# The last four F blocks of half one as one Strassen group, and their row tiles kept in DRAM until half two

## The chip, the cores and the metric

The kernel runs on one core of a Trainium2 chip. The metric is the time of one execution in microseconds of the device. The times below are medians of several executions; the profile is of one execution. Of the engines, PE multiplies matrices (PEld loads its weights), DVE and ACT work on SBUF and PSUM, POOL (GpSimd) on SBUF alone, and SP issues DMAs; ACT and POOL can issue DMAs too.

## The reference, cut to what matters

```python
x = A_x                                     # (1, 2048, 576), float32
xn = layernorm(x)
s = A_ref(xn, A_wqkv, A_w_phi, A_wo)        # linear attention, 32 heads of 18
b = (silu(xn @ B_w_gate) * (xn @ B_w_up)) @ B_w_down   # 576 -> 4608 -> 576
return x + s * silu(b)
```

The change touches the line of b (its last product, by B_w_down) and the last one. Every product runs in a split form: each float32 operand is a high part and a rest, and three products (high-high, high-rest, rest-high) are summed.

## The kernel before, in words

The 2048 rows are two halves of 1024 (`i` = 0 and 1, "half one" and "half two"). The 4608 columns of the gate are 36 F blocks of 128 (`NF`). The first part of the kernel normalizes, does the attention (its result s goes to `s_dram`) and, beside it, six F blocks of gate and up for both halves, whose h goes to `h_dram`. The second part, from about 500 us on, is one loop over `units`: for each half its 36 blocks in a fixed order, `n` being the place in it. Half two begins with a stored block, and every fourth of its first blocks is a stored one.

**Gate and up.** `gate_up` makes h of one block for the 1024 rows, as two pieces h[0] and h[1] of 512, with seven Strassen-Winograd products, `product` (L570), over the operand tiles X00 to X13. It has four PSUM tiles: two `px`, one `py`, one `pw`. ACT copies px out (`snap`, L599), DVE adds pw to such a copy (L604), ACT takes the Silu of py (L615) and px (L625), and DVE multiplies to h[1] (L626) and h[0] (L630, which is put into the list `anchor`). Products S3, A22 and S4 write px and pw again after those copies and additions. `operands(1)` reloads all seven X tiles for half two.

**Down.** h of all blocks is multiplied by rows of B_w_down and summed over the blocks. Two blocks ("a pair") and two row pieces form 2 x 2 matrices, and the product of a pair is done by seven Strassen products p1 to p7 (`strassen`), each with its own sum: `acc[:, 0..3]`, the two of `pair_sums` (P1 and P6, in an X tile) and `last_sum` (P7). Normally two pairs, four blocks, form a group, so that one PSUM tile `pd` takes both pairs before it is added to its sum (L794; the first group of a half is copied by ACT instead). Matmuls of the down part are L669. `combine` (L811) turns the seven sums into the four quarters of the result, in place in `acc`: part 0 after p6, part 1 after p3.

The last four blocks of a half (n = 32 to 35) are different. Blocks 32 and 33 are a Strassen group of a single pair. `combine` follows. Blocks 34 and 35 are multiplied in the plain form (`plain`, L672): for each of eight row tiles of 128 rows ACT copies the tile's sum from `acc` into `pd` (L690), PE adds the plain products, and ACT takes the Silu out of `pd` (L698). In half one that Silu goes back into `acc` and from there by a DMA from ACT's queue to `y_dram` (L699). In half two `finish` multiplies by s, adds x and stores.

The row tiles of half one are finished in half two, one behind every second block from n = 15 on, by `late_finish` (L645): y from `y_dram` into the tile `ts` (one buffer), s and x into `ld` (two buffers), DVE multiplies and adds (L653, L654) after the latest anchor, SP stores (L655).

**The order.** The down work lies in `queue`. `gate_up` calls `fill` at four points between its products, a stored block twice; `fill` runs items of the queue until it has done `share` pairs' worth (2, from n = 31 on 3) and leaves `LAG` = 3 behind. `look` prepares the next items (subtractions on POOL, splits into high part and rest on ACT and DVE). Over this program order a planner puts the instructions of each engine in an order of its own, by costs that it assumes and by priorities; on the chip every engine then takes its instructions in that order and waits on semaphores. `tc.issue_after(x)` keeps instructions behind x in that order.

Of the kernel before, what the change touches and what calls it, by code (L numbers as in the profile page):

```python
# [9 lines left out]
F32 = mybir.dt.float32  # L10
F32R = mybir.dt.float32r
AF = mybir.ActivationFunctionType
# [5 lines left out]
P = 128  # L18
# [3 lines left out]
HT = HS // P  # L22
NF = F // P
HALF = D // 2
# [22 lines left out]
def gated_hedgehog_kernel(ctx: ExitStack, tc, x, w_qk, w_v, w_phi, wo, w_gu, w_tail, w_down, ident_in, mask_in, out):  # L47
# [5 lines left out]
    nc = tc.nc  # L53
# [3 lines left out]
    def split(hi, lo, src):  # L57
        nc.scalar.copy(hi, src)  # L58
        nc.vector.tensor_sub(lo, src, hi)  # L59
# [7 lines left out]
    dram = ctx.enter_context(tc.tile_pool(name="dram", bufs=1, space=bass.MemoryType.DRAM))  # L67
# [6 lines left out]
    w_dram = dram.tile([NF - EARLY, P, 7, 4, P], F32, name="w_dram")  # L74
    t_dram = dram.tile([TAILS, 4, 3, 32, 7, P], F32, name="t_dram")
    a_dram = dram.tile([3, P, 5, BT], F32, name="a_dram")
    y_dram = dram.tile([HT, P, 2, HALF], F32, name="y_dram")

    def block(t):
        return t // HT, (t % HT) // 4, slice((t % 4) * P, (t % 4 + 1) * P)  # L80
# [42 lines left out]
    with ExitStack() as att:  # L123
# [8 lines left out]
        with ExitStack() as kst:  # L132
# [4 lines left out]
            with ExitStack() as pst:  # L137
# [104 lines left out]
                for n in range(6):  # L242
                    k, c = divmod(n, 3)
# [265 lines left out]
    acc = fp.tile([P, 4, HT // 2, HALF], F32, name="acc")  # L509
# [68 lines left out]
    def split_h(src):  # L578
        t = fp.tile([P, 2, BT], F32R, name="hh", bufs=4)
        split(t[:, 0], t[:, 1], src)  # L580
        return t

    def stored(src, fill):
        h = h_tile()
        for r in range(2):
            nc.sync.dma_start(h[r], src[:, r * BT:(r + 1) * BT])
        for _ in range(2):
            fill()
        return h
# [44 lines left out]
    def halves_of(ap):  # L634
        return ap.rearrange("p (a n) -> p a n", a=2)

    def finish(t, k, pd, sx, eng):
        r0 = HS + t * P
        a = acc[:, t // 4 * 2:t // 4 * 2 + 2, t % 4][:, k]
        nc.scalar.activation(a, pd, AF.Silu)  # L640
        nc.vector.tensor_mul(a, a, halves_of(sx[:, 0])[:, k])  # L641
        eng.tensor_add(a, a, halves_of(sx[:, 1])[:, k])  # L642
        nc.sync.dma_start(halves_of(of[r0:r0 + P, :])[:, k], a)

    def late_finish(t):  # L645

        y = fw.tile([P, D], F32, name="ts")
        sx = fw.tile([P, 2, D], F32, name="ld", bufs=2)
        r = slice(t * P, t * P + P)
        nc.sync.dma_start(halves_of(y), y_dram[t])  # L650
        for m, src in enumerate((s_dram, xf)):
            nc.sync.dma_start(sx[:, m], src[r, :])
        nc.vector.tensor_mul(y, y, sx[:, 0])  # L653
        nc.vector.tensor_add(y, y, sx[:, 1])  # L654
        nc.sync.dma_start(of[r, :], y)  # L655

    def final_rows(n):
        name = ("X02", "X00", "X01", "X03")[3 - n]
        t = xpool.tile([P, 2, 2, D], F32, name=name)
        r = slice(HS + 2 * n * P, HS + 2 * n * P + 2 * P)  # L660
        for m, src in enumerate((s_dram, xf)):
            nc.sync.dma_start(t[:, :, m], src[r, :].rearrange("(a p) n -> p a n", p=P))
        return t

    def three(ps, hs, ws, first):
        for n, (h, w) in enumerate((a, b) for b, a in zip(ws, hs)):
            mm = ((h[0], w[0]), (h[0], w[1]), (h[1], w[0]))
            for m, (l, r) in enumerate(mm):
                nc.tensor.matmul(ps, l, r, start=first and n == 0 and m == 0, stop=n == len(hs) - 1 and m == 2,  # L669
                                 skip_group_check=True)  # L670

    def plain(i, fs, hr, final):  # L672

        ws = []

        def weights():
            raw = fw.tile([P, 2, D], F32, name="ld", bufs=2)
            for n, f in enumerate(fs):
                nc.sync.dma_start(raw[:, n], w_down[f * P:(f + 1) * P, :])
            for n in range(2):  # L680
                w = fq.tile([P, 2, D], F32R, name="dw", bufs=3)
                split(w[:, 0], w[:, 1], raw[:, n])
                ws.append(w)

        def tile_of(t, hs):
            pd = fps.tile([P, 2, 512], F32, name="pd", bufs=2)
            fine = i == 1 and t == HT // 2 - 1
            c = slice(t % 4 * P, t % 4 * P + P)
            a2 = acc[:, t // 4 * 2:t // 4 * 2 + 2, t % 4]
            nc.scalar.copy(pd[:, :, 0:HALF], a2)  # L690
            for k in range(2):
                n = slice(k * HALF, (k + 1) * HALF)
                three(pd[:, k, 0:HALF], [(h[:, 0, c], h[:, 1, c]) for h in hs], [(w[:, 0, n], w[:, 1, n]) for w in ws],
                      False)
                if fine:
                    finish(t, k, pd[:, k, 0:HALF], final[t // 2][:, t % 2], nc.vector)
            if i == 0:
                nc.scalar.activation(a2, pd[:, :, 0:HALF], AF.Silu)  # L698
                nc.scalar.dma_start(y_dram[t], a2)  # L699
            elif not fine:  # L700
                finish(t, slice(0, 2), pd[:, :, 0:HALF], final[t // 2][:, t % 2], (nc.vector, nc.gpsimd)[t % 2])

        for r in (1, 0) if i else (0, 1):
            hs = []

            def prep(r=r, hs=hs):
                if not ws:
                    weights()
                hs += [split_h(hr[n][r]) for n in range(2)]

            queue.append([2, prep, [(2, lambda t=4 * r + t, hs=hs: tile_of(t, hs)) for t in range(4)]])
# [3 lines left out]
    def pair_sums(i):  # L715
        if (i, 0) not in extra:
            extra[i, 0] = xpool.tile([P, 2, HT // 2, HALF], F32, name="X02")
        return extra[i, 0]

    def last_sum(i):  # L720
        if (i, 1) not in extra:
            extra[i, 1] = fp.tile([P, HT // 2, HALF], F32, name="sx")
        return extra[i, 1]
# [87 lines left out]
    def combine(i, part, final):  # L811
        P1, P6, P7 = pair_sums(i)[:, 0], pair_sums(i)[:, 1], last_sum(i)
        C11, C12, C21, C22 = (acc[:, n] for n in range(4))
        if part == 0:
            nc.vector.tensor_add(P6, P6, P1)
            nc.vector.tensor_add(P7, P7, P6)
            nc.gpsimd.tensor_add(P6, P6, C22)
            nc.vector.tensor_sub(C21, P7, C21)
            nc.vector.tensor_add(C22, C22, P7)
            for k in (3, 2)[0:2 * i]:  # L820
                final[k] = final_rows(k)
        else:
            nc.gpsimd.tensor_add(C11, C11, P1)
            nc.vector.tensor_add(C12, C12, P6)  # L824
            for k in (1, 0)[0:2 * i]:
                final[k] = final_rows(k)

# [6 lines left out]
    queue, anchor, share = [], [], [2]  # L834
# [31 lines left out]
    est.close()  # L866
    fq = ctx.enter_context(tc.tile_pool(name="fq", bufs=1, reuse_waits="tile"))
    fps = ctx.enter_context(tc.tile_pool(name="fps", bufs=1, space=PSUM, reuse_waits="tile"))
    finals, late = {}, list(range(HT))
    for i, n, f in units:  # L870
        share[0] = 2 if n < RUSH else 3
        if i == 1 and n == 0:
            xo = operands(1)
        if f >= EARLY:
            w = kept.pop() if i and kept else ready.pop(0)
            if (i, f) == (0, NF - 1):
                kept.append(w)
            if todo and (i, f) != (0, NF - 1):
                ready.append(gate_up_weights(*todo.pop(0)))
        h = stored(h_dram[i, f], fill) if f < EARLY else gate_up(w, xo, fill, (i, f) == (0, EARLY))  # L880
        if n % 2 == 0:
            g = {"f": (f, units[units.index((i, n, f)) + 1][2]), "h": [h]}
            if n % 4 == 0:
                group = []
            if n < NF - 2:
                group.append(g)
        else:
            g["h"].append(h)
        if n >= NF - 2:
            if n % 2:  # L890
                plain(i, g["f"], g["h"], finals)
            continue
        if n >= NF - 4 or n % 4 > 1:
            strassen(i, group, n % 2, n < 4)
        if n % 2 == 0:
            continue
        if i and n >= 15 and late:
            with tc.issue_after(anchor[-1].ins):
                late_finish(late.pop(0))
        if n == NF - 3:  # L900
            for k in range(2):
                queue.insert(len(queue) - 2 + 3 * k,
                             [0, None, [(0, lambda i=i, k=k: combine(i, k, finals))]])
# [37 lines left out]
```

## Time and profile before

| | |
|---|---|
| median of three runs | 1647.22 us (1646.2 to 1649.27) |
| the profiled execution's own time | 1648.95 us |
| its span, first to last instruction | 1647.0 us |
| mean granted clock of PE | 0.998 |
| PE busy | 1613.3 us, 98% of the span |
| DVE, ACT, POOL busy | 1178.3, 715.3, 618.7 us |
| matmuls L669 (128 x 288) | 3048 |
| moved by DMA | 264.68 MB, mean 161 GB/s |

The profile is of one execution. Busy time is the union of an engine's instructions; idle time before an instruction is put down to what released it. A matmul's duration is its latency, and matmuls overlap, so their rate is read from one start to the next.

### The profile page before, as it was taken

To read this page: it belongs to the slowest core of one execution; us is meant where nothing else is said; L and a number is where in the kernel's file an instruction comes from. 1 tells how busy PE (TensorE), PEld (TensorE's weight loads), DVE (VectorE), ACT (ScalarE), POOL (GpSimd) and SP (SyncE) were. 2 spreads that over 40 slices of the span, in tenths; PEclk is the share of its full clock that TensorE was granted. 3 is DMA by queue.
4 is the path that set the end of the run, shared out by engine and by line. 5 is a ranking of instruction groups with operands and counts; after the bars stand their busy time and mean duration, and the time that the engine had idled before them with its cause. 6 is when DMAs were issued, how large, how long until landed. Compare 5 with 4: busy or idle time off the path is not lost.

```text
span 1647.0 us, 25211 instructions
## 1 busy us (share of the span) xinstructions
PE 1613.3 (98%) x9441; PEld 1436.0 (87%) x9441; DVE 1178.3 (72%) x1722; ACT 715.3 (43%) x1389; POOL 618.7 (38%) x660
## 2 busy tenths in 40 slices
PE   6999999999999999999999999999999999999998
PEld 5899998999987688888888888888888888888887
DVE  7677758989852476887887778844666677566578
ACT  5533345443431365444544445445433333333334
POOL 3467500343202344554554453422333244133132
PEclk9999999999999999999999999999999999999999
DMA  9623303343218545455455454495545556455435
GB/s 285 215 79 103 116 34 105 92 142 117 74 45 289 204 159 191 161 175 181 171 176 176 173 179 164 132 361 170 164 127 161 174 167 216 152 183 187 141 114 172
DMA packets 118107, 264.68 MB, mean 161 GB/s; under 512 B 12418, under 2 KB 48386, under 8 KB 116194
## 3 DMA queue, kind: packets, MB, share of 16 engines
q1 hardware_dynamic: 107628, 247.44, 45.0%
q0 software_dynamic: 3072, 11.02, 2.4%
q10 hardware_dynamic: 7286, 4.63, 0.9%
q8 instruction: 74, 1.21, 0.3%
q14 instruction: 47, 0.39, 0.1%
HBM read 164.21 MB, written 98.83 MB: 160 GB/s over the span
## 4 chain that ended last, share of the span: by engine, by line
PE 66%; DVE 2%; issue 1%; DMA 0%; POOL 0%; ACT 0%; SPq 0%; DVEq 0%; POOLq 0%
PE pd L669 24%; PE px L570 23%; PE pw L570 11%; PE py L570 6%; PE pe L92 2%; DVE acc L641 0%; DVE hh L59 0%; DMA hb<-h_dram 0%; DMA X<-s_dram 0%; DVE dw L59 0%; DVE w L59 0%; DVE ha L630 0%; DVE acc L642 0%; DVE s L604 0%; DVE acc L824 0%
## 5 line engine op out<-in xcount | busy, mean ns | idle before, releaser
L669 PEld LDWEIGHTS pd<-dw,hh 128*128 128x128 f32 x3048 | 431.9, 189 | 28.4 <-DVE dw L59 5.4
L669 PE MATMUL pd<-dw,hh 128*128 128x288 f32 x3048 | 448.3, 297 | 5.7 <-DVE dw L59 4.0
L570 PE MATMUL px<-X,w 128*128 128x512 f32 x1440 | 373.5, 393 | 1.5 <-ACT w L58 1.0
L570 PEld LDWEIGHTS px<-X,w 128*128 128x128 f32 x1440 | 261.3, 188 | 52.7 <-ACT s L599 3.5
L570 PE MATMUL pw<-X,w 128*128 128x512 f32 x720 | 185.5, 393 | 0.0
L570 PEld LDWEIGHTS pw<-X,w 128*128 128x128 f32 x720 | 134.7, 188 | 30.3 <-DVE s L604 0.3
L604 DVE TENSOR_TENSOR s<-pw,s 128x512 f32<-128x512 f32 x120 | 82.5, 687 | 102.6 <-ACT s L599 91.8
L92 PE MATMUL pe<-X,wh 128*128 128x512 f32 (+1 forms) x480 | 152.1, 400 | 1.7 <-POOL X L199 0.7
L794 DVE TENSOR_TENSOR acc<-pd,acc 128x576 f32<-128x576 f32 x128 | 96.1, 751 | 77.9 <-PE pd L669 77.8
L599 ACT COPY s<-px 128x512 f32<-128x512 f32 x120 | 70.3, 586 | 155.1 <-PE px L570 154.9
L59 DVE TENSOR_TENSOR hh<-ha,hh 128x512 fp32r<-128x512 f32 x140 | 115.5, 850 | 14.8 <-ACT hh L58 13.8
L58 ACT CAST hh<-ha 128x512 fp32r<-128x512 f32 x140 | 82.7, 619 | 95.4 <-PE pd L669 72.2
L92 PE MATMUL p<-KVWH,X 128*128 128x288 f32 (+1 forms) x640 | 123.6, 298 | 0.4 <-DVE phi L274 0.4
L766 POOL TENSOR_TENSOR hb<-hb 128x512 f32<-128x512 f32 x34 | 46.4, 1364 | 164.1 <-DVE hb L626 163.6
L92 PEld LDWEIGHTS pe<-X,wh 128*128 128x128 f32 (+1 forms) x480 | 88.5, 189 | 19.7 <-DVE h L120 1.5
L92 PEld LDWEIGHTS p<-KVWH,X 128*128 128x128 f32 (+1 forms) x640 | 100.5, 188 | 1.1 <-issue 0.8
L59 DVE TENSOR_TENSOR w<-ld,w 128x512 fp32r<-128x512 f32 (+1 forms) x90 | 76.2, 847 | 31.9 <-ACT w L58 30.5
L570 PE MATMUL px<-X,wt 96*128 96x512 f32 x240 | 94.8, 395 | 0.0
L570 PE MATMUL py<-X,w 128*128 128x512 f32 x360 | 94.0, 394 | 0.1
L779 POOL TENSOR_TENSOR ha<-ha 128x512 f32<-128x512 f32 x34 | 52.4, 1556 | 109.5 <-DVE hh L59 109.5
L58 ACT CAST w<-ld 128x512 fp32r<-128x512 f32 (+1 forms) x90 | 49.4, 549 | 87.5 <-POOL ld L560 55.2
L753 POOL TENSOR_TENSOR h<-ha,hb 128x512 f32<-128x512 f32 x34 | 45.4, 1334 | 100.7 <-DVE ha L630 66.6
(181 smaller groups left out, 3044.1 us busy)
## 6 DMA issues: line engine op xcount, KB each, us to landing
w_dram<-w SPq DMA_DIRECT2D x87, 512.0 KB, 2.8
w<-w_dram SPq DMA_DIRECT2D x87, 512.0 KB, 4.4
wt<-t_dram SPq DMA_DIRECT2D x59, 336.0 KB, 3.5
ld<-in_B_w_gu SPq DMA_DIRECT2D x30, 512.0 KB, 4.5
X<-sum_dram SPq DMA_DIRECT2D x8, 1280.0 KB, 6.8
rt<-in_B_w_down SPq DMA_DIRECT2D x33, 288.0 KB, 3.9
rb<-in_B_w_down SPq DMA_DIRECT2D x33, 288.0 KB, 4.0
w_dram<-w SPq DMA_DIRECT2D x29, 256.0 KB
```

The lines of the kernel that those rows point to most:

```text
L58: nc.scalar.copy(hi, src)
L59: nc.vector.tensor_sub(lo, src, hi)
L92: nc.tensor.matmul(ps, l, r, start=n == 0, stop=n == len(pairs) - 1)
L570: nc.tensor.matmul(ps, l, r, start=first and n == 0, stop=last and n == len(mm) - 1, skip_group_check=True)
L599: nc.scalar.copy(t, ps)
L604: nc.vector.tensor_add(t, ps, t)
L669: nc.tensor.matmul(ps, l, r, start=first and n == 0 and m == 0, stop=n == len(hs) - 1 and m == 2, skip_group_check=True)
L753: sub(s, g["h"][0][0], g["h"][0][1])
L766: nc.gpsimd.tensor_add(a21, a21, g["h"][1][1])
L779: sub(a12, a12, g["h"][0][0])
L794: nc.vector.tensor_add(a2, pd[:, :, 0:HALF], a2)
```

## The change

In half one the blocks n = 32 to 35 become one ordinary Strassen group of two pairs. `plain` is then used in half two alone. `combine` of half one moves behind that group, and its result, the sums themselves without a Silu, is stored by `keep`: four DMAs of 128 x 1152 from GpSimd's queue, two behind part 0 and two behind part 1. `y_dram` is laid out as `acc` is. In half two `late_rows` loads a row tile's y, s and x one step (two blocks) ahead of its `late_finish`, which now takes the Silu on ACT, outside of the `issue_after` that holds the multiplication and the addition.

```diff
-    y_dram = dram.tile([HT, P, 2, HALF], F32, name="y_dram")
+    y_dram = dram.tile([4, P, 4 * HALF], F32, name="y_dram")
...
-    def late_finish(t):
-
+    def late_rows(t):
         y = fw.tile([P, D], F32, name="ts")
         sx = fw.tile([P, 2, D], F32, name="ld", bufs=2)
-        r = slice(t * P, t * P + P)
-        nc.sync.dma_start(halves_of(y), y_dram[t])
+        r, c = slice(t * P, t * P + P), slice(t % 4 * HALF, (t % 4 + 1) * HALF)
+        nc.sync.dma_start(halves_of(y), y_dram[t // 4 * 2:t // 4 * 2 + 2, :, c].rearrange("k p n -> p k n"))
         for m, src in enumerate((s_dram, xf)):
             nc.sync.dma_start(sx[:, m], src[r, :])
-        nc.vector.tensor_mul(y, y, sx[:, 0])
-        nc.vector.tensor_add(y, y, sx[:, 1])
+        return r, y, sx
+
+    def late_finish(r, y, sx):
+        nc.scalar.activation(y, y, AF.Silu)
+        with tc.issue_after(anchor[-1].ins):
+            nc.vector.tensor_mul(y, y, sx[:, 0])
+            nc.vector.tensor_add(y, y, sx[:, 1])
         nc.sync.dma_start(of[r, :], y)
...
-            if i == 0:
-                nc.scalar.activation(a2, pd[:, :, 0:HALF], AF.Silu)
-                nc.scalar.dma_start(y_dram[t], a2)
-            elif not fine:
+            if not fine:
                 finish(t, slice(0, 2), pd[:, :, 0:HALF], final[t // 2][:, t % 2], (nc.vector, nc.gpsimd)[t % 2])
...
     def combine(i, part, final):
...
+        def keep(*ns):
+            for n in ns:
+                nc.gpsimd.dma_start(y_dram[n], acc[:, n].rearrange("p t n -> p (t n)"))
+
         if part == 0:
...
             nc.vector.tensor_add(C22, C22, P7)
+            if i == 0:
+                keep(2, 3)
...
             nc.vector.tensor_add(C12, C12, P6)
+            if i == 0:
+                keep(0, 1)
...
-            if n < NF - 2:
+            if i == 0 or n < NF - 2:
                 group.append(g)
...
-        if n >= NF - 2:
+        if i and n >= NF - 2:
             if n % 2:
-                plain(i, g["f"], g["h"], finals)
+                plain(g["f"], g["h"], finals)
             continue
-        if n >= NF - 4 or n % 4 > 1:
+        if n % 4 > 1 or (i and n >= NF - 4):
             strassen(i, group, n % 2, n < 4)
         if n % 2 == 0:
             continue
-        if i and n >= 15 and late:
-            with tc.issue_after(anchor[-1].ins):
-                late_finish(late.pop(0))
-        if n == NF - 3:
+        if i and n >= 13:
+            if rows:
+                late_finish(*rows.pop())
+            if late:
+                rows.append(late_rows(late.pop(0)))
+        if n == (NF - 1, NF - 3)[i]:
```

More of the change, by code (lines that the diff above doesn't have):

```diff
@@ L670, in three, with plain @@
                                  skip_group_check=True)
-    def plain(i, fs, hr, final):
+    def plain(fs, hr, final):
         ws = []
@@ L686, in tile_of @@
             pd = fps.tile([P, 2, 512], F32, name="pd", bufs=2)
-            fine = i == 1 and t == HT // 2 - 1
+            fine = t == HT // 2 - 1
             c = slice(t % 4 * P, t % 4 * P + P)
@@ L696, in tile_of @@
                     finish(t, k, pd[:, k, 0:HALF], final[t // 2][:, t % 2], nc.vector)
-            if i == 0:
-                nc.scalar.activation(a2, pd[:, :, 0:HALF], AF.Silu)
-                nc.scalar.dma_start(y_dram[t], a2)
-            elif not fine:
+            if not fine:
                 finish(t, slice(0, 2), pd[:, :, 0:HALF], final[t // 2][:, t % 2], (nc.vector, nc.gpsimd)[t % 2])
-        for r in (1, 0) if i else (0, 1):
+        for r in (1, 0):
             hs = []
@@ L868, in gated_hedgehog_kernel @@
     fps = ctx.enter_context(tc.tile_pool(name="fps", bufs=1, space=PSUM, reuse_waits="tile"))
-    finals, late = {}, list(range(HT))
+    finals, late, rows = {}, list(range(HT)), []
     for i, n, f in units:
```

## The prediction

> **What bounds the kernel now.** I read the page first, then a table of busy time by stretch, then what PE waits for, then the timelines of the places that the change touches.
>
> ```profile
> span 1647.0 us, 25211 instructions
> PE 1613.3 (98%) x9441; PEld 1436.0 (87%) x9441; DVE 1178.3 (72%) x1722; ACT 715.3 (43%) x1389; POOL 618.7 (38%) x660
> ...
> 1068.00:1136.00 68.00, 68.00 (x368) 59.33 (x367) 33.61 (x46) 33.97 (x62) 16.47 (x12) 1.00 0.85 304
> 1136.00:1590.00 454.00, 454.00 (x2507) 401.56 (x2506) 293.60 (x426) 174.83 (x347) 142.23 (x119) 1.00 0.52 162
> ...
> PE pd L669 <- DVE X L794: 0.4, 1, 0.4
> ```
>
> The two middle rows are the table by stretch (length; then busy time and count of PE, PEld, DVE, ACT, POOL). From 1068 to 1136 us, where half one goes over into half two, PE is busy all 68.00 us, and in half two from 1136 to 1590 all 454.00. The last row is all that PE waits for between 900 and 1300 in the view of waits. So PE is the bound: a matmul that goes is worth its time, and a delay of another engine costs nothing until PE waits for it, and from there on all of it.
>
> **Matmuls removed.** In the plain form the last pair of F blocks of half one costs 96 matmuls of 288 columns (8 row tiles, 2 column halves, 2 blocks, 3 terms). As the second pair of a Strassen group it adds 84 (7 products, 4 row tiles, 3 terms). 12 go, and the order in which the changed kernel is built shows just that.
>
> ```profile
> 1090.81 1.76 PE L669 MATMUL pd<-dw,hh 128*128 128x288 f32 x12
> 1092.40 1.53 PE L570 MATMUL px<-X,w 128*128 128x512 f32 x6
> 1094.01 1.76 PE L669 MATMUL pd<-dw,hh 128*128 128x288 f32 x12
> 1052.53 1.06 PE L669 MATMUL pd<-dw,hh 128*128 128x288 f32 x6 [0.44 <-DVE X L794]
> 1085.91 3.22 PEld L669 LDWEIGHTS pd<-dw,hh 128*128 128x128 f32 x24 [0.33 <-ACT pd L690]
> ...
> L669 PE MATMUL pd<-dw,hh 128*128 128x288 f32 x3048 | 448.3, 297 | 5.7 <-DVE dw L59 4.0
> ```
>
> Twelve such matmuls take 1092.40 - 1090.81 = 1.59 us from start to next start (the mean of 297 ns in the last row, from the groups, is the latency of one; they are pipelined). That is the whole gain in work: **-1.6 us**. In brackets stand two waits of PE in the single pair and the plain pair: 0.44 and 0.33 us. Both forms are gone, so I count **-0.8 us** for them. At most the change thus brings 2.4 us, 0.15%. About 0.2% (3.3 us) is what a measurement of this kernel can tell from no change.
>
> **Work moved beside PE.** ACT loses eight copies into PSUM, eight Silus and eight store issues around 1088 to 1121 us and gets three more splits of h and some small ones of weights, DVE the same splits, POOL eight more additions and subtractions of the second pair and four store issues. ACT's 33.97 and DVE's 33.61 busy us of 68 in the first table row cover that, so in sum it costs nothing. The stores on POOL wait for the last sums; behind them stand one sum (needed only by a store and by the next group's first product, 20 us of PE work later) and preparations of the next group, so this hides too. The first read of y stands on SP ahead of the weights of block 6, and each later read two blocks earlier than before, behind the same store: what is queued there is for a block ahead. I count nothing for it. What is left is the order on ACT and DVE.
>
> **The combine.** In the changed order the sums of Strassen's products (lines L815 to L824 of the kernel before) stand on DVE between the last item of product p6 and the addition of pw and the snapped px (L604) of block 2 of half two. PE's product S4 overwrites pw and waits for that addition. Before, other items lay between, and PE shows no wait there.
>
> ```profile
> 1059.61 0.69 DVE L59 TENSOR_TENSOR hh<-ha,hh 128x512 fp32r<-128x512 f32 x1
> 1062.00 0.75 DVE L794 TENSOR_TENSOR acc<-pd,acc 128x576 f32<-128x576 f32 x1
> 1062.67 0.45 DVE L59 TENSOR_TENSOR dw<-rb,dw 128x288 fp32r<-128x288 f32 x1
> 1065.28 1.35 DVE L815 TENSOR_TENSOR X<-X 128x1152 f32<-128x1152 f32 x1
> 1066.55 0.68 DVE L604 TENSOR_TENSOR s<-pw,s 128x512 f32<-128x512 f32 x1
> 1068.34 1.94 DVE L816 TENSOR_TENSOR sx<-sx,X 128x1152 f32<-128x1152 f32 x1
> 1070.36 2.68 POOL L817 TENSOR_TENSOR X<-X,acc 128x1152 f32<-128x1152 f32 x1 [1.29 <-DVE sx L816]
> 1070.88 3.38 DVE L818 TENSOR_TENSOR acc<-sx,acc 128x1152 f32<-128x1152 f32 x1
> 1074.18 1.35 DVE L819 TENSOR_TENSOR acc<-acc,sx 128x1152 f32<-128x1152 f32 x1
> ```
>
> From the end of p6's last item DVE must do: an add (0.75), two splits (0.69 each), the first sum (1.35), a split of weights (0.45), the second sum (1.94, or 1.35 beside an idle POOL), an add (0.75), the third sum, which took 3.38 us beside POOL's 2.68, the fourth (1.35) and the addition (0.68): 11.4 to 12.0 us, less 0.7 because neighbours overlap by 0.08 (1065.28 + 1.35 against 1066.55). With 0.2 to start, that is 11.2 on the middle. PE meanwhile has 28 matmuls of 512 columns and 24 of 288 until S4: 28 x 0.23 (seven in 1094.01 - 1092.40) + 24 x 0.133 = 9.6 us. **+1.6 us.** Bounds: nothing, if POOL doesn't meet the third sum (it then takes 1.35), and 2.5. I take the row with POOL, because its addition is again released by the second sum, just ahead of the third.
>
> **A load pulled close.** In the changed order two matmuls of half two's first gate stand 6.1 us of PE work (21 x 0.23 + 11 x 0.133, less 0.2 for the reader's own end) behind the last reader of that X tile, and the tile must be reloaded between.
>
> ```profile
> X<-a_dram SPq DMA_DIRECT2D x3, 1280.0 KB, 7.0
> ```
>
> Its 7.0 us would give 1.0 us of waiting; but that median had other loads ahead of it, which now stand behind. **+0.3 us**, between 0 and 1.0.
>
> **The late Silus.** This is the largest term. In half two each row tile of half one is read back (y_dram to "ts"), gets its Silu on ACT, is multiplied and added on DVE after an anchor, and stored. There is one buffer "ts": the next read waits on SP until the store has landed. Only the DVE part is tied to the anchor. The Silu isn't, and in the changed order it stands on ACT early, apparently where the planner thought the read would be there: the third (block 18), fifth, sixth, seventh and eighth between py's Silu (L615) and the snap of px (L599). ACT takes its queue in order, and behind the twelve 288-column matmuls PE waits for that snap.
>
> ```profile
> 1305.76 0.34 SPq L655 DMA_DIRECT2D out<-ts  x1
> 1309.29 0.32 SPq L650 DMA_DIRECT2D ts<-y_dram  x1
> ...
> 1327.26 0.34 SPq L655 DMA_DIRECT2D out<-ts  x1
> 1329.91 0.32 SPq L650 DMA_DIRECT2D ts<-y_dram  x1
> ...
> 1455.14 0.34 SPq L655 DMA_DIRECT2D out<-ts  x1
> 1457.42 0.32 SPq L650 DMA_DIRECT2D ts<-y_dram  x1
> ...
> 1486.17 0.34 SPq L655 DMA_DIRECT2D out<-ts  x1
> 1489.89 0.33 SPq L650 DMA_DIRECT2D ts<-y_dram  x1
> ```
>
> These are rows of SP's timeline, out<-ts a store and ts<-y_dram the next read; the next ones are of ACT and PE.
>
> ```profile
> 1087.87 0.65 ACT L698 ACTIVATE acc<-pd 128x576 f32<-128x576 f32 x1 [0.94 <-PE pd L669]
> ...
> 1315.24 1.56 PE L570 MATMUL px<-X,w 128*128 128x512 f32 x6
> 1329.96 0.58 ACT L615 ACTIVATE py<-py 128x512 f32<-128x512 f32 x1 [0.17 <-PE py L570]
> 1331.56 0.59 ACT L599 COPY s<-px 128x512 f32<-128x512 f32 x1 [1.02 <-PE px L570]
> 1332.96 1.56 PE L570 MATMUL px<-X,w 128*128 128x512 f32 x6
> 1492.81 1.56 PE L570 MATMUL px<-X,w 128*128 128x512 f32 x6
> ```
>
> The stores and reads are issued in the changed kernel in the same places behind the same DVE additions, so the kernel before tells when. The next read is issued 2.3 to 3.7 us after the store (3.53, 2.65, 2.28 and 3.72 in the rows; seven cases, mean 3.1): that is the landing of 288 KB. No view shows the landing of the reads; the nearest rows for 288 KB are these, and 3.9 for the loads of x in a busier place:
>
> ```profile
> ld<-in_A_x SPq DMA_DIRECT2D x8, 288.0 KB, 3.9
> ```
>
> I take 3.1, because it is the same tile, place and size. Third Silu: read issued at 1329.91, landed at 1333.0, Silu 0.65 (as L698), snap 0.59, 0.1 for hand-overs: PE may go on at 1334.35, where it went on at 1332.96. It waits 1.4 us. Eighth: 1489.89 + 4.44 = 1494.3 against 1492.81, 1.5 us. The five distances from read to PE are 3.05, 3.45, 3.37, 3.01 and 2.92 us; 5 x 4.44 less their 15.8 is **+6.4 us**. The second and fourth stand ahead of py's Silu with a stored block between: 1309.29 + 3.1 + 0.65 + 0.58 + 0.59 + 0.1 = 1314.3, before the 1315.24 at which PE wants it; nothing. Bounds: a landing of 2.3 leaves 2.4 us, one of 3.9 makes 10.4.
>
> **The sum.** -1.6 - 0.8 + 1.6 + 0.3 + 6.4 = +5.9 us. The profiled execution took 1648.95 us (span 1647.0), 1.7 above the median of the three runs, 1647.22; the change is the same on both: 1654.9 for the former, **1653.1** for the median.
>
> **Rivals.** *The reads are there in time, and the combine hides* (not slower). It decides at a landing of 2.3 us and a third sum without POOL: then 2.4 + 0 + 0 - 2.4 = 0, 1647.2; with the combine's 1.6 still there, 1648.8. For it: the fastest store landed in 2.3. Against it: the mean of seven is 3.1, and to hide all five a landing under 1.6 is needed, faster than any row. 0.19.
>
> *The stores from GpSimd come late, and the first Silu blocks ACT as well.*
>
> ```profile
> y_dram<-acc ACTq DMA_DIRECT2D x8, 288.0 KB, 4.8
> t_dram<-th POOLq DMA_DIRECT2D x64, 112.0 KB, 2.8
> DMA to landing us min/median/max: 2.1/2.8/6.5
> ```
>
> The last store waits for the last sum (0.75 + 1.38 + 1.35 us after p3), then landing, read 3.1, Silu 0.65 and two more steps of ACT (1.3), about 8.6 us beside the landing; PE has 35 x 0.23 + 48 x 0.133 = 14.4 us of work until it wants the result. So a landing up to 5.8 us is hidden. The rows have 4.8 for 288 KB in the crowded switch, 2.8 for 112 KB from GpSimd and 6.5 as the worst. Here 576 KB go at once: at 7 to 8.4 us the price is 1.2 to 2.6, 1654.3 to 1655.7. 0.11. [...]
>
> *The change doesn't do what it says*: the built order has the 12 matmuls fewer, the four stores and the eight Silus; I leave 0.01.
>
> **How the numbers follow.** The forecast has 0.69. Its own range is 1649.1 to 1657.1 by the landing of the reads. The range 1648.0 to 1658.0 adds the late stores, the bounds of the combine and the upper part of the first rival, and leaves out what lies below. Slower than 1650.5 are the late stores (0.11) and the forecast but for its fastest landings (0.66): 0.77. Faster than 1643.9 would need no wait at all and more than the 2.4 us of gain: 0.02 of the first rival. Within 0.2% is the rest, 0.21.
>
> **What would show it.** In the profile after: 3036 matmuls of L673 in place of 3048; waits of PE px for "ACT s L599", some five of 1 to 2 us, in half two; ACT's Silu of ts right behind a DMA's landing; one wait of pw for DVE s L604 near 1110 us; PE busy less than the whole from 1136 on. Wrong if PE stays without waits after 1136, or if the reads land within 2 us.

## The result, and the profile after

The changed kernel takes **1667.87 us** (median of four, 1666.48 to 1671.06), the kernel before on the same chip 1648.05 (four, 1646.2 to 1649.27): a ratio of 1.0120, 95% interval 1.0108 to 1.0133. It is slower, as forecast, but by 19.8 us and not by 5.9; the range ended at 1658.0.

From the page of the changed kernel (span; busy time of the engines; the matmuls of the down part):

```profile
span 1669.3 us, 25210 instructions
PE 1617.6 (97%) x9429; PEld 1436.6 (86%) x9429; DVE 1184.1 (71%) x1730; ACT 712.3 (43%) x1389; POOL 634.1 (38%) x672
...
L673 PE MATMUL pd<-dw,hh 128*128 128x288 f32 x3036 | 447.5, 297 | 5.8 <-DVE dw L59 4.0
```

The 12 matmuls are gone (3036). PE's busy time is not shorter but 4.3 us longer, which is a first sign: some matmuls ran slower. The table by stretch (length; busy time and count of PE, PEld, DVE, ACT, POOL; granted clock, DMA share, GB/s), with the two stretches shown of before:

```profile
1068.00:1136.00 68.00, 63.03 (x335) 55.07 (x335) 46.46 (x61) 23.43 (x46) 29.68 (x22) 0.95 0.73 250
1136.00:1590.00 454.00, 444.65 (x2442) 392.04 (x2441) 280.40 (x413) 177.81 (x352) 135.73 (x114) 1.00 0.53 162
```

PE was busy all 68.00 and 454.00 us; now 5.0 and 9.4 are missing, and in the switch the granted clock is 0.95 on average. What PE waits for from 500 us on, with total, number and longest (of the seven waits in the first row, five are the late Silus'):

```profile
PE px L570 <- ACT s L599: 9.7, 7, 2.6
PE pw L570 <- DVE s L604: 4.9, 1, 4.9
...
PE py L570 <- ACT py L611: 1.3, 1, 1.3
...
PE pd L673 <- ACT sx L793: 0.5, 1, 0.5
```

To see which part of the 19.8 us lies where, the same instruction can be followed through both traces: ACT's Silu of py (L615), which both run 60 times. Three of them before, and the same three after:

```profile
1038.36 0.58 ACT L615 ACTIVATE py<-py 128x512 f32<-128x512 f32 x1
...
1160.59 0.58 ACT L615 ACTIVATE py<-py 128x512 f32<-128x512 f32 x1
...
1541.48 0.58 ACT L615 ACTIVATE py<-py 128x512 f32<-128x512 f32 x1 [1.74 <-PE py L570]
```

```profile
1040.95 0.58 ACT L615 ACTIVATE py<-py 128x512 f32<-128x512 f32 x1
...
1171.24 0.58 ACT L615 ACTIVATE py<-py 128x512 f32<-128x512 f32 x1
...
1563.84 0.58 ACT L615 ACTIVATE py<-py 128x512 f32<-128x512 f32 x1 [1.74 <-PE py L570]
```

The distance is 2.59 us before the change begins (it is set ahead of 600 us, and over the traces of all kernels here lies between -1.9 and +2.7: the scatter of the kernel's first part), then 10.65 and 22.36. So the switch from half one to half two costs 8.1 us and the late Silus in half two 11.7. The prediction had -0.5 and +6.4.

**The switch.** PE's timeline of the changed kernel:

```profile
1114.17 0.39 PE L570 MATMUL px<-X,wt 96*128 96x512 f32 x1
1119.44 2.93 PE L570 MATMUL pw<-X,w 128*128 128x512 f32 x6 [4.88 <-DVE s L604]
1122.17 0.63 PE L570 MATMUL pw<-X,wt 96*128 96x512 f32 x1
1122.60 2.48 PE L673 MATMUL pd<-dw,hh 128*128 128x288 f32 x12
1124.91 1.54 PE L570 MATMUL px<-X,w 128*128 128x512 f32 x6
```

PE waits 4.88 us for the addition of pw. Then six matmuls of 512 columns take 2.73 us to the next start, where they take 1.38 elsewhere (1124.91 to 1126.29), and twelve of 288 take 2.31 in place of 1.60. The reason is in the table of 4 us steps, in the third column from the end:

```profile
1112.00:1116.00 4.00, 2.56 (x15) 1.94 (x13) 2.17 (x3) 1.87 (x4) 3.92 (x3) 1.00 0.13 22
1116.00:1120.00 4.00, 0.56 (x1) 0.50 (x2) 2.57 (x4) 0.00 (x0) 2.44 (x3) 0.67 0.48 192
1120.00:1124.00 4.00, 4.00 (x13) 3.39 (x12) 4.00 (x5) 0.00 (x0) 3.86 (x2) 0.50 0.57 172
1124.00:1128.00 4.00, 4.00 (x21) 3.45 (x21) 3.92 (x7) 1.11 (x2) 2.54 (x4) 0.98 0.93 335
```

The granted clock is 0.50 (in steps of 0.2 us: from 1117.4 to 1124.2). I call what PE loses from one start to the next, less 0.2315 us for each 512-column and 0.1332 for each 288-column matmul (in undisturbed rows seven take 1.62 us and twelve 1.60), its loss: 5.04 us at the wait and 2.25 behind it by the clock. Why the wait is so long is seen on DVE and POOL:

```profile
1106.14 0.81 POOL L755 TENSOR_TENSOR td<-rb,rt 128x288 f32<-128x288 f32 x1 [4.80 <-DMA rb<-in_B_w_down]
...
1110.28 1.96 DVE L822 TENSOR_TENSOR sx<-sx,X 128x1152 f32<-128x1152 f32 x1
...
1112.83 1.34 DVE L824 TENSOR_TENSOR acc<-sx,acc 128x1152 f32<-128x1152 f32 x1
1112.99 1.83 POOL L761 TENSOR_TENSOR td<-rb,rt 128x288 f32<-128x288 f32 x1
1114.79 2.60 POOL L823 TENSOR_TENSOR X<-X,acc 128x1152 f32<-128x1152 f32 x1
1117.43 1.36 DVE L825 TENSOR_TENSOR acc<-acc,sx 128x1152 f32<-128x1152 f32 x1 [3.25 <-POOL X L823]
1118.70 0.68 DVE L604 TENSOR_TENSOR s<-pw,s 128x512 f32<-128x512 f32 x1
```

The second sum (L822) is done at 1112.24. GpSimd's sum of X and acc (L823) could go then, but GpSimd is in the six preparations of the next group's weights (the first and the last are shown), which had waited for a load of "rb" until 1106. It starts at 1114.79. The fourth sum on DVE (L825) overwrites the part of acc that GpSimd's sum reads, so it waits 3.25 us, and the addition of pw (L604) stands behind it.

**Half two.** One of the five late Silus, with the read, the Silu and the snap on ACT, and PE's matmul that waited for it:

```profile
1342.32 0.37 SPq L649 DMA_DIRECT2D ts<-y_dram  x1
1345.17 0.68 ACT L655 ACTIVATE ts<-ts 128x576 f32<-128x576 f32 x1 [3.97 <-DMA ts<-y_dram]
1345.76 0.57 ACT L599 COPY s<-px 128x512 f32<-128x512 f32 x1
1346.38 2.93 PE L570 MATMUL px<-X,w 128*128 128x512 f32 x6 [2.60 <-ACT s L599]
```

The mechanism is the predicted one: the Silu stands on ACT ahead of the snap, and waits for the read's landing (here 2.85 us). The five waits are 2.60, 1.21, 1.31, 1.89 and 1.86 us, 8.87 in all (9.65 as PE's loss), and the first brings a half clock too: its six matmuls take 2.93 us.

### The profile page after: what moved, and what is told of

It reads as the page before. It is cut to its first block, busy times and chain, and to the rows that moved or that the text cites. A ratio compares the mean times of both kernels' runs of the same rounds, so it can differ in the third digit from the quotient of the medians.

```text
span 1669.3 us, 25210 instructions
## 1 busy us (share of the span) xinstructions
PE 1617.6 (97%) x9429; PEld 1436.6 (86%) x9429; DVE 1184.1 (71%) x1730; ACT 712.3 (43%) x1389; POOL 634.1 (38%) x672
## 3 DMA queue, kind: packets, MB, share of 16 engines
q8 instruction: 74, 1.21, 0.3%
## 5 line engine op out<-in xcount | busy, mean ns | idle before, releaser
L604 DVE TENSOR_TENSOR s<-pw,s 128x512 f32<-128x512 f32 x120 | 82.5, 688 | 98.1 <-ACT s L599 89.7
```

Of the source, the lines that this page charges most:

```text
L604: nc.vector.tensor_add(t, ps, t)
```

## Experiments

The theories. **A**: each wait costs PE its length, and a long one a spell of half clock besides; the waits come from the order on ACT (late Silus) and on DVE and GpSimd (sums), and go when that order goes. **B**: the new transfers disturb PE, and the order only shows where. **C**: the sums cost PE about the same wherever they stand, since DVE has no room in the switch. **D**: the half clock has nothing to do with the waits. In the change only DVE's part of the late rows has an anchor; experiment 1 gives the Silu one on ACT. Each ratio is to the kernel before run beside it (medians 1648.9 to 1650.3 us).

**1. The Silus behind an anchor on ACT.**

```diff
-            nc.scalar.activation(xp, xp, AF.Silu)
+            behind.append(nc.scalar.activation(xp, xp, AF.Silu))
...
-        nc.scalar.activation(y, y, AF.Silu)
+        with tc.issue_after(behind[-1].ins): nc.scalar.activation(y, y, AF.Silu)
```

> The changed kernel with one edit: ACT's Silu of each row that is read back is queued behind the Silu of px (L625) of the block in which the row is finished, two blocks after its read is issued. Only ACT's order changes; all other engines keep theirs. Theory A (the late Silus block ACT, and each wait costs PE its length, plus a spell of half clock after a long one): PE's six waits for ACT s L599 in half two (8.9 us), the half-clock spell after the longest (1.5 us) and the wait for sx (0.7 us with its restart) go, and nothing comes in their place: 1667.9 - 11 = 1657 us, between 1655 and 1659. Theory B (the reads and stores of half two disturb PE by their traffic, and ACT's order is only where it shows): the same transfers stay, so PE waits elsewhere, and the time stays within 3 us of 1667.9.

Measured: 1656.16 us, ratio 1.0046 (1.0031 to 1.0062). PE's waits from 1000 us on, the whole list:

```profile
PE pw L570 <- DVE s L604: 4.9, 1, 4.9
PE py L570 <- ACT py L611: 1.3, 1, 1.3
PE pd L673 <- ACT pd L694: 0.7, 1, 0.7
PE pd L673 <- ACT acc L640: 0.6, 1, 0.6
```

No wait for ACT s is left; the last two are at the end, as before. With the same transfers in half two its 11.7 us are gone (by the Silus of py). B falls there, and the time is within 1 us of A's 1657.

**2. The first half's sums behind an anchor on DVE, alone and with edit 1.**

```diff
+        if wait:
+            with tc.issue_after(anchor[-1].ins): combine(0, wait.pop(), finals)
...
-                             [0, None, [(0, lambda i=i, k=k: combine(i, k, finals))]])
+                             [0, None, [(0, lambda i=i, k=k: wait.append(k) if i + k == 0 else combine(i, k, finals))]])
```

> The changed kernel with one edit: the four sums of the first half's combine are queued on DVE behind the multiplication that ends block 2 of half two, so that the addition of pw (L604) no longer stands behind them. The Silus stay as in the changed kernel. Theory A (the 4.9 us wait is the queue on DVE and POOL, and the half clock follows from the wait): the wait of pw (4.9), the half-clock spell behind it (2.3) go, and the sums hide beside PE's work: 1667.9 - 7 = 1661 us, between 1659 and 1663. Rival C (the sums must be done soon in any case, since the next group's copies into the same tiles wait for them): a wait of pd or of DVE comes in its place and less than 3 us is won. Rival D (the half clock does not hang on the wait): a spell of half clock stays near 1117 us.

> Both edits at once: the Silus behind their anchor on ACT, the first half's sums behind theirs on DVE. Theory A: what is left of the change is its 12 fewer matmuls (-1.6), the two waits of before that are gone (-0.8) and the wait of 1.4 us for py's copy near 1053 us that the changed order brought: 1648 - 1 = 1647 us, between 1645 and 1650. If the two costs are not independent (theory B or rival C), it stays over 1653.

Measured: alone 1665.35 us (1.0100, 1.0086 to 1.0114), with edit 1 1654.20 (1.0029, 1.0018 to 1.0041). Only 2 to 3.4 us are won (each against the kernel before beside it), not 7: C is nearer. PE waits in the first of them:

```profile
PE px L570 <- ACT s L599: 6.7, 5, 1.9
PE pd L673 <- DVE acc L795: 2.5, 1, 2.5
```

The wait for pw has become one of 2.5 us for the addition of pd into acc, behind the same sums, again with a spell of half clock.

**3. The third sum (L823, on GpSimd after the change) on DVE.**

```diff
-            nc.gpsimd.tensor_add(P6, P6, C22)
+            (nc.gpsimd if i else nc.vector).tensor_add(P6, P6, C22)
```

> The changed kernel with one edit: the third sum of the first half's combine (X plus acc, L823) runs on DVE instead of GpSimd. Theory A (the wait of pw was long because GpSimd's sum stood behind six preparations of weights there): from the end of the second sum DVE does an add, the third and fourth sum and the addition of pw, 0.75 + 1.35 + 1.35 + 0.68 us, 1.9 for each sum while GpSimd runs beside it; so the wait is 1.7 to 2.9 us in place of 4.9, and the time 1660 to 1665 us. Rival (the sums are late for another reason, GpSimd's queue is not it): the wait stays near 4.9 and the time at 1668.

Measured: 1664.26 us (1.0094, 1.0079 to 1.0109). The wait for pw is 2.13 us, inside the expected 1.7 to 2.9: having this sum on GpSimd made the other 2.75. That is not the price of GpSimd's queue alone, as the sum takes 1.34 us on DVE in place of 2.60, and in this kernel's order the addition of pw stands ahead of the fourth sum, no longer behind it. The queue's own share is read from the rows after the change: the sum started 2.55 us after L822 was done (1112.24 to 1114.79). By the Silus of py the switch costs 4.5 us in place of 8.1. The profiled execution (1666.52 us) gains less, since the late Silus cost 14.7 us in it (11.7 after the change, 9.0 in the first kernel of experiment 2), with ACT's order the same in all three but for one swapped pair. Two of this trace's waits show why:

```profile
1398.45 1.99 PE L570 MATMUL px<-X,w 128*128 128x512 f32 x6 [1.77 <-ACT s L599]
1400.24 0.63 PE L570 MATMUL px<-X,wt 96*128 96x512 f32 x1
...
1438.81 1.64 PE L570 MATMUL px<-X,w 128*128 128x512 f32 x6 [3.12 <-ACT s L599]
1440.29 0.40 PE L570 MATMUL px<-X,wt 96*128 96x512 f32 x1
```

A wait of 1.77 us has slow matmuls behind it, one of 3.12 us has none. The last section comes back to this.

**4. The late Silu alone, on the kernel before.** Half one stores its plain pair's sums without their Silu, and half two takes it as in the changed kernel.

```diff
-                nc.scalar.activation(a2, pd[:, :, 0:HALF], AF.Silu)
+                nc.scalar.copy(a2, pd[:, :, 0:HALF])
```

and `late_rows` and `late_finish` as in the change.

> The kernel before, with the late Silu alone: half one stores the plain pair's sums without their Silu (a copy by ACT in its place, stored from ACT as before), and half two reads, applies the Silu on ACT, multiplies, adds and stores as in the changed kernel. No Strassen group is changed. Theory A (the late Silu's cost does not hang on the grouping): five waits of PE px for ACT s of 1.2 to 2.6 us, and a spell of half clock behind the longest: 1648.9 + 8 to 11 = 1657 to 1660 us. Rival (the late Silus only block since the group's sums and stores come late): under 1652 us.

Measured: 1656.05 us (1.0045, 1.0031 to 1.0058), +6.8, below the expected range. PE waits 5.2 us for ACT s, in four:

```profile
PE px L570 <- ACT s L599: 5.2, 4, 1.8
```

The longest is 1.80 us and no spell of half clock follows. So the late Silu needs no grouping to cost, and its cost is not a fixed one.

**5. Waits made to measure.** The snap of px repeated k times in nine blocks of the kernel before.

```diff
-                nc.scalar.copy(t, ps)
+                for _ in range(1 + more):
+                    nc.scalar.copy(t, ps)
```

> The kernel before, in which the snap of px in nine blocks of half two is done k extra times over (0.57 us each on ACT), with k = 3, 4, 6, 8, 10 and 12, 7, 9 in blocks far apart, to make PE wait a set time. The snap of before ends 0.8 us ahead of PE's need, so the waits should be about 0.57 k - 0.8: 0.9, 1.5, 2.1 (k = 5), 2.6, 3.8, 4.9, 6.0, 3.2 and 4.3 us, 29 us in all. Theory A (the granted clock is set for whole stretches of 3.4 us on a fixed grid, by PE's activity in the stretch before): no spell after 0.9 and 1.5, one of 3.4 or 6.8 us after all waits of 3.2 and more, and after 2.1 and 2.6 by where they fall on the grid; each spell costs half its busy part, 1 to 3 us, so the whole is 1648 + 29 + 10 to 16 = 1687 to 1693 us. Rival D (the clock falls for another reason): no spells, or spells away from the waits, and 1677 us.

Measured once: 1658.18 us. It tells nothing on the clock: the planner counted these copies in, and put other matmuls ahead of the waiting ones:

```profile
1353.22 6.95 PE L671 MATMUL pd<-dw,hh 128*128 128x288 f32 x51
```

51 down matmuls stand in a row, at a place where the kernel before has 12; PE waits 0.9 us in all for ACT s, and there is no spell. The 7.1 us by which half two is longer come in many small steps. A late DMA is what the planner does not foresee.

**6. The sums cut in two, with edit 1.** The first two sums stay, the other two and GpSimd's (on DVE) wait for the anchor; what waits is issued by the two lines `if wait:` of experiment 2. Then also the last subtraction of the last block's weights on DVE, which moves py's copy ahead on ACT.

```diff
+            if i == 0 and part == 0:
+                wait.append(2)
+                return
+            (nc.gpsimd if i else nc.vector).tensor_add(P6, P6, C22)
...
-            nc.gpsimd.tensor_sub(ld[:, 1], ld[:, 1], ts[:, 1])
+            (nc.vector if f == NF - 1 else nc.gpsimd).tensor_sub(ld[:, 1], ld[:, 1], ts[:, 1])
```

> The changed kernel with the Silus behind their anchor on ACT, and the combine cut in two: the first two sums stay where they are, the other two and GpSimd's (now on DVE) are queued behind the multiplication that ends block 2. Theory A: the first two are done before S4 needs DVE, as they were at 1112 us, and the rest is beside work that PE has in hand; no wait of over 0.5 us is left near 1110 to 1135, only that for py's copy near 1050 (1.4 us): -1.6 - 0.8 + 1.4 and about 0.9 of small gaps, so 1649 us, 1647 to 1651. Rival C (the sums cost PE some 4 us wherever they stand, since DVE has no room here beside GpSimd): a wait for another reader comes, and the time is 1652 or more.

> As the split combine with the Silus behind their anchor, and the last subtraction of the last block's weights (L560) on DVE instead of GpSimd, which puts py's copy ahead of that weight's split on ACT. Theory A: the wait of 1.4 us near 1050 goes as well: 1647.5 us, 1646 to 1649, the same as before or just faster. Rival: another wait comes in its place, and the time is that of the split combine.

Measured: 1650.26 us (1.0012, 1.0003 to 1.0021) and 1649.94 (1.0007, 0.9998 to 1.0016). The waits for pw are 0.18 us, that for py goes in the second; one of 0.96 for a split of h is left. DVE and POOL in the second:

```profile
1109.98 3.05 POOL L835 TENSOR_TENSOR acc<-acc,X 128x1152 f32<-128x1152 f32 x1 [0.67 <-DVE acc L795]
1110.42 3.30 DVE L59 TENSOR_TENSOR dw<-td,dw 128x288 fp32r<-128x288 f32 x2
...
1115.56 3.90 DVE L827 TENSOR_TENSOR X<-X,acc 128x1152 f32<-128x1152 f32 x1
1115.69 1.30 POOL L772 TENSOR_TENSOR ha<-hb,ha 128x512 f32<-128x512 f32 x1
1116.94 1.29 POOL L754 TENSOR_TENSOR h<-ha,hb 128x512 f32<-128x512 f32 x1
...
1121.31 1.35 DVE L829 TENSOR_TENSOR acc<-acc,sx 128x1152 f32<-128x1152 f32 x1
```

A sum that takes 1.35 us takes 3.90 beside two operations of GpSimd of 1.30 and 1.29, and two splits, 0.82 elsewhere, take 3.30 beside one of 3.05. In these rows DVE stood still while GpSimd worked.

**7. Both ways from there: the third sum back on GpSimd; none of the sums on GpSimd.**

```diff
-            nc.gpsimd.tensor_add(C11, C11, P1)
+            (nc.gpsimd if i else nc.vector).tensor_add(C11, C11, P1)
```

> As the split combine with the Silus behind their anchor and the last subtraction of the weights on DVE, but with the third sum (X plus acc) back on GpSimd, where it stands ahead of the other sum of GpSimd near 1108 us. Theory A: DVE has 1.35 us less to do between block 2's last multiplication and the split of h that PE waited 0.96 us for, so that wait goes and nothing is left in the switch: 1649 us, 1647.5 to 1650, the same as before by what can be measured or just below it. Rival (DVE stands still while GpSimd works, so moving the sum there costs DVE as much elsewhere): a wait of about 1 us or more in another place near 1110 to 1125, and 1650 or more.

> As the split combine with the Silus behind their anchor and the last subtraction of the weights on DVE, and the first half's last GpSimd sum (acc plus X, C11) on DVE as well, so that GpSimd does none of the sums. Theory E (DVE and GpSimd take turns at these operations on two operands in SBUF, so a sum on GpSimd costs DVE all its 3 us): DVE gets 1.35 us more of its own and loses the 2.4 us by which its two splits of weights near 1110 stood still (3.30 us in place of 0.82 to 0.9), so DVE is done about 1 us earlier, the wait of 0.96 us for the split of h shrinks or goes, and the time is 0.5 to 1 us under that kernel's 1649.9: 1649, 1647.5 to 1650. Rival (GpSimd's work is done beside DVE's): DVE is 1.35 us later, the wait grows to 2 us, and the time is 1651 or more.

Measured: 1651.75 us (1.0015, 1.0006 to 1.0025) and 1648.93 (0.9994, 0.9985 to 1.0003). With the sum on GpSimd a wait of 2.17 us is back, with a spell of half clock: the rival. With none there, PE's list of waits from 1000 to 1640 us is one row, at the end:

```profile
PE pd L673 <- ACT pd L694: 0.7, 1, 0.7
```

So C held for the sums in one piece beside GpSimd, not for the sums themselves. This is the best version of the change, and it can't be told from the kernel before.

## Why the prediction was too low

The direction and the places were right; two terms of the sum were mis-sized, and two costs were not in it. In us, by PE's losses:

| step | predicted | measured |
|---|---|---|
| 12 matmuls fewer, two waits gone | -2.4 | -2.4 by counts; -1.4 in the trace of the last kernel, which has no new wait |
| combine, wait of pw | +1.6 (0 to 2.5) | +5.0 |
| late Silus, waits | +6.4 (2.4 to 10.4) | +9.7 |
| X tile pulled close | +0.3 | 0, no wait for X |
| work moved beside PE | 0 | py +1.4; first Silu +0.7 |
| half clock behind the waits | not in it | +2.25 and +1.5 |
| sum | +5.9 | +18.2, and 1.6 not placed; the traces say 19.8 |

The prediction's second wait of PE, 0.33 us, stands in a row of the weight load (PEld). PE's own starts in the kernel before show 0.17 us lost there and 0.71 at the first wait, so the -0.8 holds.

**Combine.** The failed step is "its addition is again released by the second sum, just ahead of the third": the prediction took from the kernel before that GpSimd is idle there. In the changed order six preparations, released by a late load, stood ahead of it. The prediction had even counted GpSimd's new work as hidden: it asked what stands behind GpSimd's stores, and not what stands ahead of its sum. The sum that the prediction calls the third, DVE's (L824), took 1.34 us, less than the 3.38 assumed; it was the fourth that waited, for GpSimd's. The queue held GpSimd's sum back by 2.55 us; without that the loss would have been some 2.5 us (5.04 - 2.55, an estimate), the upper bound of the forecast. With that sum on DVE (experiment 3) the wait was 2.13.

**Late Silus.** The mechanism, the places (third, fifth to eighth) and the missing waits of the second and fourth are as forecast, and alone on the kernel before they cost 6.8 us by the times and 6.2 by the trace, where the forecast had 6.4. That nearness is partly luck: four waits of 0.54 to 1.80 us made it up there, not the five of 1.0 to 1.5 that the forecast adds up. In the changed kernel the five reads landed after 2.85, 3.37, 3.01, 4.76 and 3.03 us (sum 17.0; 15.5 assumed). And the reads were issued only 13.4 us in all ahead of PE's need (15.8 assumed), the first 1.3 in place of 3.05, since it followed the store ahead of it by 4.75 us (2.65 in the row that was used). So what failed here is the size of the landing ("I take 3.1, because it is the same tile, place and size") and of the head start, not the mechanism; differences in either go one to one into PE's wait: from the landing to PE's start it is 1.21 us each of the five times, and 17.0 + 5 x 1.21 - 13.4 is the 9.65 that PE lost.

**Work beside PE.** The wait for py's copy (1.28 us at 1053.72) comes from ACT's split of a weight that GpSimd had not yet subtracted; experiment 6 took it away. The rival of the late stores came true in small: the first read was issued 6.65 us after the last store from GpSimd (1140.27 and 1133.62), the first Silu blocked ACT, and PE waited 0.49 us for "ACT sx". GpSimd's four stores landed after 3.09, 3.08, 4.25 and 6.60 us: only the last was later than the 5.8 us that the prediction took as hidden.

**The clock** was not in the prediction in any form: 3.8 us, a fifth of the loss.

## What to carry to other kernels

Where one engine is busy all the time, a saving of work is worth that work, and a wait that the change brings can cost more than its length (here 0.1 to 0.2 us to start again, and up to 2.25 of half clock behind it); so look first for work that an in-order engine must do between the bottleneck's own steps, and put nothing there that hangs on a DMA's landing (2.85 to 4.76 us for the five reads). A wait has to be costed by what stands ahead of it in the queue of each engine in the chain, with that engine's late loads, as the order of the kernel before does not carry over. Of two engines that take turns, as DVE and GpSimd did here, the sum of both is the time (3.94 us by their operations, 3.90 measured).

## What the runs showed of the hardware

**The granted clock fell after waits of under 2 us, and by a fixed grid.** All spells of half clock in a trace begin on a grid of 3.413 us: after the change at 1117.37 and 1346.06 (228.69 us, 67 steps apart), in experiment 3 at 1112.86, 1338.14 and 1399.58 (225.28 and 61.44 us, 66 and 18 steps). I cut five traces into these stretches and read PE's busy time in each from 1000 to 1600 us. In a stretch behind one with 1.65 us of busy time or less (nine cases, 0 to 48%) the clock was 0.50. Behind one at full clock with 1.68 or more (the waits of 1.2 to 3.1 us, 49% and up) it stayed 1.00. After a stretch at half clock with 1.34 and 1.99 us busy the half clock stayed, with 3.03 and more it ended. That explains the two rows of experiment 3: the 3.12 us wait was cut by a border and left 1.97 and 1.73 us of work in its two stretches, the 1.77 us wait left 1.65. D falls. So the length of a gap alone did not decide: the one of 1.77 us brought a spell that cost about 1.6 us more (seven matmuls of 512 columns and twelve of 288 took 4.86 us, 3.22 elsewhere), the one of 3.12 none.

One and the same wait can go either way. Near 573 us, ahead of all that the edits touch, PE waits 1.51 to 1.53 us in each of the twelve traces. In three of them (the second kernel of experiment 2, both of experiment 7) half clock follows. The wait, and the next eight matmuls of the down part, in the kernel before and in the last kernel of experiment 7:

```profile
573.22 0.66 PE L669 MATMUL pd<-dw,hh 128*128 128x288 f32 x3 [1.53 <-DVE dw L59]
574.19 1.33 PE L669 MATMUL pd<-dw,hh 128*128 128x288 f32 x8
...
573.34 0.66 PE L673 MATMUL pd<-dw,hh 128*128 128x288 f32 x3 [1.51 <-DVE dw L59]
574.59 2.12 PE L673 MATMUL pd<-dw,hh 128*128 128x288 f32 x8
```

These three spells stand behind stretches with 1.82 to 1.84 us busy (53 to 54%), so the busy time of the view has no border that holds everywhere. It counts the last matmul of each run of work with its whole latency. If 0.165 us is left off the end of each run (a latency of 0.297 less a step of 0.133), the stretches at full clock from 500 us on sort in all twelve traces: behind 1.51 us or less the clock was 0.50 (18 cases), behind 1.65 or more it was 1.00. This border is read out of these cases afterwards and was not tried with set waits.

**DVE and GpSimd took turns.** The rows of experiment 6 add up: 1.30 + 1.29 + 1.35 = 3.94 against the 3.90 of the sum. The one that started first did not keep its turn: DVE's sum is recorded 0.13 us ahead of GpSimd's first operation, and ended after both. GpSimd can be the one that waits: after the change its preparation at 1112.99 took 1.83 us beside DVE's sum of 1.34, where the same line took 0.81 in the kernel before (1068.26). One addition with an operand in PSUM kept its time beside GpSimd: pd into acc, 0.74 us at 1112.16 after the change (0.75 in the mean of all 128), beside a preparation of 1.81 at 1111.10.

**Open:** why a read could follow the store of 288 KB ahead of it after 2.28 us in one place and only after 5.01 in another, and the 1.6 us that the table does not place; gaps of about 0.1 us at short runs of matmuls are more frequent in the changed order, and make about half of it.
